# Where the first MoE 1 steps and the last weight conversions stand in chunk 1 of an attention and MoE kernel

## The chip, the cores and the metric

One core of a Trainium2 chip. The metric is the device time of one execution in microseconds, the median of several runs. Engines are named as the profile names them: PE (TensorE) with its weight loads PEld, DVE (VectorE), ACT (ScalarE), POOL (GpSimd), and SP, whose queue issues the DMAs. Each engine, and each DMA queue, takes its instructions in the order in which the program wrote them.

## The reference

Three stages run one after the other, all in float32 (the weights of the two MoE stages come as 8-byte values):

```python
for t in range(768):                       # 4 batches x 8 heads, state 40 x 40
    y[:, :, t] = einsum('bhd,bhde->bhe', rt, state)
    Sa = einsum('bhde,bhe->bhd', state, at)
    state = state * wt - outer(Sa, bt) + outer(vt, kt)
x = y as [3072, 320]
h = x @ w_in                               # MoE 1: 320 -> 2048 -> 320
x = (h * clip(h + 3, 0, 6) / 6) @ w_out
out = ((x @ w_a) * (x @ w_b)) @ w_out2     # MoE 2: 320 -> 1536 -> 320
```

## The kernel before

**Attention.** The 768 steps are cut into 12 chunks of 64, and `window(j)` lists the steps of chunk j. A chunk's recurrence is turned into small matmuls and one triangular solve. `op_a(j + 1, 0)` and `op_a(j + 1, 1)` (L474) make the scores of the next chunk: 64 matmuls each on PE (L484), two copies of the diagonal blocks to AB on ACT (L487) and two masked copies on DVE (L491). `t_load(j + 1)` (L498) sends AB through memory into the layout of the solve (`scr`, then `TA`; L504, L507), and `t_start(j + 1)` runs the solve on POOL (L518, L521). One window later `t_store(j)` (L526) copies a part of the result on ACT (TA, L531), stores it (L534 to L536) and loads it back as NY and AB (L540 to L542); `merge_y(j)` (L544, matmuls L550) is the first step that needs it. After it come `merge_z`, `op_c`, `op_d`, `op_g`, `op_e`, `op_f` and `op_sd`, and with `op_b(j + 1)` (L576, matmuls L581, copies RH L582) the next window begins. POOL does nothing but solves from chunk 1 on.

**MoE 1.** Chunk j's output (256 tokens) goes through memory: `xt_move(j)` (L673) loads it back transposed, `prep(j)` (`moe1_x`, L286) splits it into xh (ACT, L290) and xl (DVE, L291), and then 8 `up` steps and 8 `down` steps follow. An `up(i)` is 16 matmuls (L311), then in turn ACT (g, L316), DVE (product, L317), ACT (gh, L132) and DVE (gl, L133). A `down(i)` is 12 matmuls (L331 to L333). They stand in one list `mq` in the order prep 0, up 0, up 1, down 0, up 2, down 1, ..., up 7, prep of the next chunk, down 6, down 7, up 0 of the next chunk, and so on. `MOE[j]` says ahead of which steps of window j the next entry of that list is issued; windows 2 to 9 have the same 16 places, two of them at 2 and 7. What is left after window 11 is issued in a loop of its own ahead of MoE 2 (L1045).

**Weights of MoE 1.** They are converted and split into two parts on the way. While `room["wide"]` holds, up to three or four pieces are in work at once; the first `xt_move` flushes them (L675) and from there on each `conv1.go()` is one narrow pass of up to 192 columns: load to `ws` (two buffers), ACT (L79), five DVE instructions (L80 to L88), ACT (L263), DVE (L265). Seven such passes are left when window 1 begins. `WEIGHTS[j]` says ahead of which steps they are issued; an entry that finds nothing to convert issues nothing.

**Order around the change.** Window 1 begins with `xt_move(0)`. Its steps 0 and 1 are `op_b(1, .)`, 2 and 3 the loads for chunk 3, 4 and 6 `op_a(2, .)`, 8 and 9 `t_load(2)` and `t_start(2)`, 11, 12, 14 and 15 `op_kbt(2, .)`, 17 `merge_y(1)`, 18 `merge_z(1)`, 22 and 23 `op_c`, 38 `op_f(1, 1)`, 41 and 42 `op_sd(2, .)`.

Of the kernel before, what the change touches and what calls it, by code (L numbers as in the profile page):

```python
# [29 lines left out]

MOE = {
    0: (),
    1: (13, 18, 18, 19, 21, 22, 26, 26, 34, 38, 39),
    **{j: (2, 7, 14, 14, 19, 20, 23, 25, 32, 34, 38, 39, 41, 45, 48, 49) for j in range(2, NCH - 2)},
    NCH - 2: (2, 5, 11, 11, 14, 15, 16, 17, 21, 23, 27, 28, 30, 34, 37, 38),
    NCH - 1: (3, 3, 3, 3, 3, 4, 6, 11, 11, 13, 13, 13, 19, 20, 23, 23, 23)}
WEIGHTS = {
    0: (0, 3, 6, 8, 10, 17, 18, 21, 22, 22, 26, 27),
    1: (1, 2, 4, 5, 10, 13, 16, 16, 33, 36)}
EARLY = NCH - 6  # L40
WCOLS = 256
STORE_1 = 25
RANGE = 7
INV_SCALE = 1.0e9

HALVES = ((0, 0), (1, 64))
# [50 lines left out]
def attention_and_moe(ctx, tc, t, flag):  # L97
# [283 lines left out]
    def setup_first():  # L381
        for q, eng in ((32, ve), (96, gp)):
            eng.memset(raw[q:q + 32], 1.0)
            eng.memset(raw[q:q + 32].rearrange("q (p t) -> q p t", p=NP)[:, :, 0:1], 0.0)
        load_kb(0)
        load_w(0)
        ve.memset(seg, 0.0)
        ve.memset(seg.rearrange("q (p t) -> q p t", p=4)[:, :, 0:1], 1.0)
        for q in (32, 96):
            gp.memset(LB[0][q:q + 32, q // 64], 0.0)  # L390
        load_a(0)
        for q in (32, 96):
            ve.memset(LB[1][q:q + 32, q // 64], 0.0)
        gp.memset(TN2, 0.0)
        make_identity(nc, ident)
        pad(KB)
        load_kb(1)
        pad(RV.rearrange("q a p c -> q (a p c)"))
        sp.dma_start(out=mask, in_=t["mask"])
        for z in n2:  # L400
            sp.dma_start(out=z.rearrange("a p s t -> (a p) s t")[:, :, 0:32], in_=TN2[0:32])
# [21 lines left out]
    def load_w(j):  # L423
        for ab, q in HALVES:
            sp.dma_start(out=raw[q:q + D], in_=t["we"][j, ab])

    def load_a(j):
        for ab, q in HALVES:
            sp.dma_start(out=LB[j % 2][q:q + D, ab], in_=t["ae"][j, ab])
# [9 lines left out]
    def load_vt(j):  # L439
        for ab, q in HALVES:  # L440
            sp.dma_start(out=VX[64 - q:128 - q, ab], in_=t["vte"][j, ab])
# [4 lines left out]
    def prep_w(j, k):  # L446
        rw = py["rw", k % 2] = a2.tile([128, 4, C], F32, tag="rw", name="rw")
        w = W[j % 3][:, 4 * k:4 * k + 4]
        ve.tensor_tensor_scan(out=w.rearrange("q p t -> q (p t)"), data0=raw[:, 260 * k:260 * k + 260], data1=seg,
                              initial=0.0, op0=ALU.mult, op1=ALU.add)  # L450
        ve.reciprocal(out=rw, in_=w[:, :, 1:65])  # L451

    def prep_a(j, eng=nc.vector, ps=slice(0, NP)):
        for ab in range(2):
            a_ = LB[j % 2][half(ab), ab, ps]
            eng.tensor_tensor(out=a_, in0=a_, in1=W[j % 3][half(ab), ps, 0:64], op=ALU.mult)
# [6 lines left out]
    def prep_kb(j, k, eng=nc.vector):  # L463
        kb = kb_of(j)[:, 4 * k:4 * k + 4].rearrange("q p (s c) -> q p s c", s=2)
        r1 = py["rw", k % 2]
        rw = r1.rearrange("q p (s c) -> q p s c", s=1)
        eng.tensor_tensor(out=kb, in0=kb, in1=rw.to_broadcast([128, 4, 2, C]), op=ALU.mult)

        square(r1, 1.0, stat[:, 8 * j + k:8 * j + k + 1])
# [4 lines left out]
    def op_a(j, hf, later=None):  # L474

        lb, AB, KB = LB[j % 2], ABs[j % 2], kb_of(j)
        p0 = 8 * hf
        pss = [bank().rearrange("q (p c) -> q p c", p=8) for _ in range(2)]
        for i in range(8):
            p = p0 + i  # L480
            for o in range(2):
                for ab in range(2):
                    c = o ^ ab
                    mm(pss[ab][half(c), i], KB[rows(ab), p, 64 * c:64 * c + 64], lb[rows(ab), ab, p],  # L484
                       start=True, stop=True)
        for ab in range(2):
            ac.copy(out=AB[half(ab), p0:p0 + 8], in_=pss[ab][half(ab)])  # L487

            def masked(ab=ab):
                o = half(1 - ab)  # L490
                ve.tensor_tensor(out=lb[o, ab, p0:p0 + 8], in0=pss[ab][o],  # L491
                                 in1=mask[o, None, :].to_broadcast([64, 8, 64]), op=ALU.mult)
            masked() if later is None else later.append(masked)
# [4 lines left out]
    def t_load(j, between=lambda: None):  # L498
        scr = dram.tile([2, 2, NP, 32, 32], F32, tag="scr", name="scr", bufs=2)
        AB = ABs[j % 2]  # L500
        for sub in range(2):
            for ab in range(2):
                r0 = 64 * ab + 32 * sub
                sp.dma_start(out=scr[sub, ab].rearrange("p s t -> s p t"),  # L504
                             in_=AB[r0:r0 + 32, :, 32 * sub:32 * sub + 32])
        between()
        sp.dma_start(out=TA2[t_half(j)], in_=scr.rearrange("u a p s t -> (u a p) s t"))  # L507
# [15 lines left out]
    def t_start(j):  # L523
        t_solve(t_half(j), gp)
# [434 lines left out]
    with tc.manual_schedule():  # L959
        gp.memset(stat, 0.0)  # L960
        setup_first()
        conv1.ahead()
        later = []
        for k in range(4):
            prep_w(0, k)
            prep_kb(0, k, gp)
            if k == 3:
                load_w(1)
                load_a(1)
            if k % 2:  # L970
                prep_a(0, ve, slice(4 * k - 4, 4 * k + 4))
                op_a(0, k // 2, later)
        t_load(0)
        setup_rest()
        load_vt(0)
        for k in range(4):
            prep_w(1, k)
            prep_kb(1, k, gp)
            later.pop(0)()
        prep_a(1)  # L980
        t_start(0)
        for hf in range(2):
            op_a(1, hf, later)
            for _ in range(2):
                conv1.go()
                later.pop(0)()

        def turn(j):
            for bk in range(4):
                op_kbt(j, bk)  # L990
                conv1.go()

        t_load(1, lambda: turn(0))
        t_start(1)
        load_w(2)
        load_kb(2)
        turn(1)
        load_rv(0)
        prep_sq(0)
        prep_sq(1)  # L1000
        conv1.go()
        t_store(0, conv1.go)

        streams = [moe1_stream(j) for j in range(NCH)]
        preps = [p for p, _, _ in streams]
        mq = [preps[0], streams[0][1][0]]
        for j, (_, ups, downs) in enumerate(streams):
            for i in range(1, 8):
                mq += [ups[i]] + (preps[j + 1:j + 2] if i == 7 else []) + [downs[i - 1]]
            mq += [downs[7]] + [u[0] for _, u, _ in streams[j + 1:j + 2]]  # L1010

        def moe_step():
            mq.pop(0)()
            while mq and mq[0] in preps:
                mq.pop(0)()

        first2, early = early2(), [0] * NCH
        for j in range(NCH):
            for f in window(j):
                if f == MOE_STEP:  # L1020
                    if j == 1 and mq[0] in preps:
                        mq.pop(0)()
                    else:
                        moe_step()
                elif f == WEIGHT and j >= EARLY:
                    early[j] += 1
                    if early[j] in (1, 4, 7):
                        next(first2, None)
                elif f == WEIGHT:
                    if conv1.todo or conv1.loaded or room["wide"]:  # L1030
                        conv1.go()
                else:
                    f[0](*f[1:])
        for _ in first2:
            pass
        at.close()
        c2 = ctx.enter_context(ExitStack())
        w2p = c2.enter_context(tc.tile_pool(name="w2", bufs=1, side="right", reuse_waits="tile"))
        xr = c2.enter_context(tc.tile_pool(name="x2", bufs=1, side="right", reuse_waits="tile"))
        left = []  # L1040
        w2 = Weights2(w2p, xr)
        load_x, trans, rest = moe2(w2, xr, lambda: left[0])
        decide = in_range()
        n = 0
        while len(mq) > 2:  # L1045
            moe_step()
            n += 1
            if n == RANGE:
                decide()
                load_x(0)  # L1050
            if n == RANGE + 5:
                trans(0)
                load_x(1)
        m1i.close()
        mq.pop(0)()
        trans(1)
        mq.pop(0)()
        m1w.close()
        left.append(c2.enter_context(tc.tile_pool(name="xl2", bufs=1, reuse_waits="tile")))
        rest()  # L1060
# [217 lines left out]
```

## Time and profile before

| | us |
|---|---|
| runs | 1282.98, 1289.79, 1292.96 |
| median | 1289.79 |
| the profiled execution | 1290.56 |
| its span, first to last instruction | 1288.7 |
| around the span | 1.9 |
| PE busy | 1099.9 (85%) |
| DVE busy | 827.2 (64%) |
| POOL busy | 470.6 (37%) |

A row of a timeline gives start and duration in microseconds, the engine, the line, the operation, what is written from what, shapes, count, and in brackets the idle time before it on its engine with what ended it.

### The profile page before, as it was taken

To read this page: it belongs to the slowest core of one execution; us is meant where nothing else is said; L and a number is where in the kernel's file an instruction comes from. 1 tells how busy PE (TensorE), PEld (TensorE's weight loads), DVE (VectorE), ACT (ScalarE), POOL (GpSimd) and SP (SyncE) were. 2 spreads that over 40 slices of the span, in tenths; PEclk is the share of its full clock that TensorE was granted. 3 is DMA by queue.
4 is the path that set the end of the run, shared out by engine and by line. 5 is a ranking of instruction groups with operands and counts; after the bars stand their busy time and mean duration, and the time that the engine had idled before them with its cause. 6 is when DMAs were issued, how large, how long until landed. Compare 5 with 4: busy or idle time off the path is not lost.

```text
span 1288.7 us, 34786 instructions
## 1 busy us (share of the span) xinstructions
PE 1099.9 (85%) x14826; PEld 1002.2 (78%) x14826; DVE 827.2 (64%) x1391; ACT 519.2 (40%) x1087; POOL 470.6 (37%) x797
## 2 busy tenths in 40 slices
PE   1213447988999998989999998999999999999997
PEld 1213336988998988979888998998888888888886
DVE  7899777565756566867777654345674775675332
ACT  1233344544554535455545554333443332332221
POOL 4789105556658484838465663000000000000000
PEclk9999857989999999999999999999999999999999
DMA  6254252333241505253433324132220110110111
GB/s 174 48 142 113 68 153 54 88 76 86 68 102 57 137 23 139 67 128 87 116 104 87 97 61 106 48 107 89 78 71 20 41 41 22 43 41 6 41 42 43
DMA packets 133858, 100.33 MB, mean 78 GB/s; under 512 B 87520, under 2 KB 121440, under 8 KB 131680
## 3 DMA queue, kind: packets, MB, share of 16 engines
q1 hardware_dynamic: 133696, 98.04, 28.0%
q8 instruction: 118, 1.93, 0.6%
q14 instruction: 44, 0.36, 0.1%
HBM read 75.13 MB, written 22.87 MB: 76 GB/s over the span
## 4 chain that ended last, share of the span: by engine, by line
PE 42%; DVE 16%; POOL 14%; DMA 11%; ACT 7%; issue 6%; SPq 3%; DVEq 0%; ACTq 0%; POOLq 0%
PE att L891 21%; POOL TN L521 7%; POOL TT L518 7%; PE up L311 4%; PE ac L915 3%; PE ac L914 3%; PE ac L913 3%; DMA KB<-in_kbe_dram 2%; DVE rw L451 2%; DMA scr<-AB 2%; DMA n<-TA 2%; PE dn L333 1%; DMA st<-in_w1o_dram 1%; PE dn L331 1%; DMA TA<-scr 1%
## 5 line engine op out<-in xcount | busy, mean ns | idle before, releaser
L518 POOL TENSOR_TENSOR TT<-TA,TN 64x31 f32<-64x31 f32 (+15 forms) x372 | 214.5, 576 | 264.2 <-DMA TA<-scr 235.8
L891 PE MATMUL att<-x2h,up 128*128 128x512 f32 x720 | 237.2, 394 | 0.0
L521 POOL TENSOR_TENSOR TN<-TN,TT 64x31 f32<-64x31 f32 (+15 forms) x372 | 224.2, 603 | 29.2
L891 PE MATMUL att<-x2l,up 128*128 128x512 f32 x432 | 170.4, 395 | 2.0 <-DVE x2l L876 2.0
L891 PEld LDWEIGHTS att<-x2h,up 128*128 128x128 f32 x720 | 135.0, 188 | 28.9
L331 PE MATMUL dn<-wo_h,gh 128*128 128x320 f32 x384 | 130.7, 340 | 13.3 <-ACT gh L132 13.3
L333 PE MATMUL dn<-wo_h,gl 128*128 128x320 f32 x384 | 124.6, 324 | 1.5 <-DVE gl L133 1.5
L332 PE MATMUL dn<-wo_l,gh 128*128 128x320 f32 x384 | 123.1, 321 | 0.0
L317 DVE SCALAR_TENSOR_TENSOR up<-g,up 128x512 f32<-128x512 f32 x96 | 66.3, 690 | 82.1 <-ACT g L316 81.9
L896 DVE TENSOR_TENSOR att<-att,asb 128x512 f32<-128x512 f32 x72 | 50.4, 700 | 97.5 <-PE att L891 80.5
L316 ACT ACTIVATE g<-up,bias 128x512 f32<-128x512 f32 x96 | 66.0, 688 | 114.0 <-PE up L311 111.5
L311 PE MATMUL up<-xh,wi_h 128*128 128x256 f32 x384 | 107.4, 301 | 3.1 <-ACT xh L290 3.1
L132 ACT CAST gh<-up 128x512 fp32r<-128x512 f32 x96 | 56.2, 586 | 129.4 <-DVE up L317 126.1
L133 DVE TENSOR_TENSOR gl<-up,gh 128x512 fp32r<-128x512 f32 x96 | 66.4, 691 | 65.1 <-ACT gh L132 65.1
L311 PE MATMUL up<-xh,wi_l 128*128 128x256 f32 x384 | 101.8, 286 | 0.0
L891 PEld LDWEIGHTS att<-x2l,up 128*128 128x128 f32 x432 | 81.1, 188 | 19.4 <-DVE x2l L876 3.5
L331 PEld LDWEIGHTS dn<-wo_h,gh 128*128 128x128 f32 x384 | 75.7, 197 | 18.1 <-ACT gh L132 14.6
L913 PE MATMUL ac<-dn,g2h 128*128 128x320 f32 x288 | 89.5, 311 | 0.0
L915 PE MATMUL ac<-dn,g2l 128*128 128x320 f32 x288 | 88.6, 308 | 0.1
L914 PE MATMUL ac<-dn,g2h 128*128 128x320 f32 x288 | 88.7, 308 | 0.0
L451 DVE RECIPROCAL rw<-W 128x256 f32<-128x256 f32 x48 | 84.2, 1753 | 3.2 <-ACT sq L461 0.2
L132 ACT CAST g2h<-att 128x512 fp32r<-128x512 f32 x72 | 42.2, 587 | 103.7 <-DVE att L896 101.7
(149 smaller groups left out, 2476.8 us busy)
## 6 DMA issues: line engine op xcount, KB each, us to landing
RV<-in_rve_dram SPq DMA_DIRECT2D x24, 320.0 KB
KB<-in_kbe_dram SPq DMA_DIRECT2D x22, 320.0 KB
st<-in_w1i_dram SPq DMA_DIRECT2D x13, 384.0 KB
raw<-in_we_dram SPq DMA_DIRECT2D x24, 162.5 KB
LB<-in_ae_dram SPq DMA_DIRECT2D x24, 160.0 KB
VX<-in_vte_dram SPq DMA_DIRECT2D x24, 160.0 KB
yt<-Y SPq DMA_DIRECT2D x48, 80.0 KB
x2d<-x SPq DMA_DIRECT2D x24, 160.0 KB
```

Of the source, the lines that this page charges most:

```text
L132: ac.copy(out=hi, in_=src)
L311: mm(u[:, e], a_, b_, start=(n == 0), stop=(n == len(seq) - 1))
L331: mm(acc, gh[:, e, c0:c0 + 128], wo_h[:, m], start=(m == 0), stop=False)
L332: mm(acc, gh[:, e, c0:c0 + 128], wo_l[:, m], start=False, stop=False)
L333: mm(acc, gl[:, e, c0:c0 + 128], wo_h[:, m], start=False, stop=(m == 15))
L451: ve.reciprocal(out=rw, in_=w[:, :, 1:65])
L518: eng.tensor_tensor(out=tv, in0=TA[:, 0:u, u:u + 1].to_broadcast([nr, u, n]), in1=TN[:, u:u + 1, u:32].to_broadcast([nr, u, n]), op=ALU.mult)
L521: eng.tensor_tensor(out=TN[:, 0:u, u:32], in0=TN[:, 0:u, u:32], in1=tv, op=ALU.subtract)
L891: mm(u, a_, b_, start=(n == 0), stop=(n == len(seq) - 1))
L913: mm(acc, gh[:, sl], w[:, 0], start=(i == 0), stop=False)
L914: mm(acc, gh[:, sl], w[:, 1], start=False, stop=False)
L915: mm(acc, gl[:, sl], w[:, 0], start=False, stop=(i == BLOCK - 1))
```

## The change

Three tables and one number of the code change. Chunk 1 gets 14 MoE 1 entries in place of 11, from step 5 on in place of step 13; its conversions stand at steps 0 to 13; the fallback decision and the first transposes for MoE 2 follow the shift in the last loop.

```diff
-    1: (13, 18, 18, 19, 21, 22, 26, 26, 34, 38, 39),
+    1: (5, 6, 8, 10, 13, 16, 18, 19, 21, 22, 26, 26, 34, 38),
...
-    1: (1, 2, 4, 5, 10, 13, 16, 16, 33, 36)}
+    1: (0, 0, 1, 2, 3, 5, 6, 8, 10, 13)}
...
-RANGE = 7
+RANGE = 5
...
-            if n == RANGE + 5:
+            if n == RANGE + 4:
                 trans(0)
```

Written out with the code's own lists, the head of window 1 is (pass = one narrow conversion):

```
before: xt_move 0 | op_b 0 | pass 1 | op_b 1 | pass 2 | loads | pass 3 | op_a 0 | pass 4 | op_a 1 |
        t_load, t_start | pass 5 | kbt 0, 1 | pass 6, prep | kbt 2, 3 | pass 7 | merge_y | up 0, up 1 |
        merge_z | down 0 | up 2 | down 1 | op_c 0, 1 | up 3, down 2 | ... | up 4 | ... | down 3 | op_f 1 | up 5
after:  xt_move 0 | passes 1, 2 | op_b 0 | pass 3 | op_b 1 | pass 4 | load | pass 5 | load | op_a 0 |
        pass 6, prep | pass 7, up 0 | op_a 1 | up 1 | t_load, t_start | down 0 | kbt 0, 1 | up 2 | kbt 2, 3 |
        down 1 | merge_y | up 3 | merge_z | down 2 | up 4 | down 3 | op_c 0, 1 | up 5, down 4 | ... | up 6 | ... |
        down 5 | op_f 1
```

All later windows take the list three entries further on at unchanged places. In windows 2 to 9, and at the like places of window 10, that puts at place 2 (behind `op_b`, ahead of `t_store`) `up 7` and the next chunk's prep where `down 4` stood, at place 7 (between the two `op_a`) `down 6` where `up 6` stood, and at place 32 (ahead of `op_g`) `up 3` where `down 0` stood. The last loop has three entries fewer (`up 6`, `down 5` and `up 7` of chunk 10 are done).

## Rows read from the trace of the kernel before

**Rows 1.** Stretch: us; busy (count) of PE, PEld, DVE, ACT, POOL; PEclk, DMA share, GB/s
```profile
183.00:204.00 21.00, 7.70 (x144) 6.39 (x144) 15.72 (x43) 8.27 (x24) 0.23 (x1) 0.50 0.46 121
```

**Rows 2.** Timeline of ACT in the head of window 1
```profile
184.39 0.37 ACT L79 ACTIVATE cv<-ws 128x192 f32<-128x192 f32 x1 [0.55 <-DMA ws<-in_w1o_dram]
191.05 0.30 ACT L263 CAST wi_h<-cv 128x128 fp32r<-128x128 f32 x1 [1.54 <-DVE cv L88]
195.00 1.18 ACT L487 COPY AB<-att 64x512 f32<-64x512 f32 x2
203.46 0.83 ACT L290 CAST xh<-xt 128x768 fp32r<-128x768 f32 x1
```

**Rows 3.** Timeline of PE there: op_a(2, 1), first matmuls of up 0 and up 1
```profile
187.30 1.98 PE L484 MATMUL att<-LB,KB 40*64 40x64 f32 x62 [2.93 <-ACT RH L582]
204.34 0.58 PE L311 MATMUL up<-xh,wi_h 128*128 128x256 f32 x1 [3.12 <-ACT xh L290]
207.92 0.41 PE L311 MATMUL up<-xh,wi_h 128*128 128x256 f32 x1
```

**Rows 4.** Timeline of POOL: first and last instruction of chunk 2's solve
```profile
203.77 0.28 POOL L518 TENSOR_TENSOR TT<-TA,TN 64x31 f32<-64x31 f32 x1 [68.53 <-DMA TA<-scr]
243.75 0.24 POOL L521 TENSOR_TENSOR TN<-TN,TT 64x31 f32<-64x31 f32 x1
```

**Rows 5.** Chain that ended last, in window 1: start, us, what (op_c; up 5)
```profile
221.56 1.99 PE att L590 x64
241.96 2.11 PE up L311 x16
```

**Rows 6.** Timeline of PE and ACT where window 2 begins
```profile
245.33 2.06 PE L581 MATMUL att<-VX,LB 128*64 128x40 f32 x64
245.60 0.58 ACT L132 CAST gh<-up 128x512 fp32r<-128x512 f32 x1 [0.76 <-DVE up L317]
249.65 2.03 ACT L531 COPY TA<-TN 32x1024 f32<-32x1024 f32 x1
```

**Rows 7.** Timelines of PE, ACT and SP where windows 3, 5 and 10 begin
```profile
306.07 2.06 PE L581 MATMUL att<-VX,LB 128*64 128x40 f32 x64
311.68 2.05 ACT L531 COPY TA<-TN 32x1024 f32<-32x1024 f32 x1 [1.19 <-POOL TN L521]
321.27 0.48 SPq L540 DMA_DIRECT2D NY<-n  x1
326.56 1.20 PE L550 MATMUL att<-NY,AB 32*32 32x32 f32 x64
...
438.11 0.48 SPq L540 DMA_DIRECT2D NY<-n  x1
440.36 1.19 PE L550 MATMUL att<-NY,AB 32*32 32x32 f32 x62 [0.79 <-DMA NY<-n]
...
726.77 2.06 PE L581 MATMUL att<-VX,LB 128*64 128x40 f32 x64
731.45 2.04 ACT L531 COPY TA<-TN 32x1024 f32<-32x1024 f32 x1
```

**Rows 8.** Waits of PE from 250 to 790 us: total us, times, longest
```profile
PE dn L331 <- ACT gh L132: 11.8, 6, 3.1
PE att L550 <- DMA NY<-n: 8.4, 6, 2.0
```

**Rows 9.** Timeline of DVE in window 4
```profile
392.82 0.70 DVE L467 TENSOR_TENSOR KB<-KB,rw 128x512 f32<-128x512 f32 x1 [5.39 <-DMA KB<-in_kbe_dram]
```

**Rows 10.** Chain that ended last, in the last loop: two up steps in succession
```profile
859.55 1.92 PE up L311 x16
863.23 1.92 PE up L311 x16
```

**Rows 11.** Stretches of window 2 and of window 7, columns as in rows 1
```profile
264.00:268.00 4.00, 4.00 (x51) 3.94 (x47) 0.76 (x1) 1.15 (x2) 0.00 (x0) 0.50 0.38 52
547.00:608.00 61.00, 54.82 (x1073) 51.18 (x1073) 45.36 (x67) 32.07 (x67) 35.42 (x60) 1.00 0.39 104
```

## The prediction

> **What bounds the kernel now.** I read the head of window 1 first, since only its order is rewritten by hand, and then the beginning of each later window, where the shift of three entries lands. In the busy times of the stretch from 183 to 204 us PE works 7.7 of 21 us, at a granted clock of 0.50, the 1.2 GHz level [rows 1]: this is the hole into which the change puts work. The timeline of POOL shows what the hole costs besides: chunk 2's solve begins at 203.77, after 68.53 us without work, and lasts until 243.99 [rows 4]. What it waits for is the second pair of AB copies, which ends on ACT at 196.18 [rows 2]; the 7.6 us from there to 203.77 are t_load's way through memory.
>
> From window 2 on two loops run side by side. One is the solve with its transfers. In the other PE waits for NY, merges, works through the window up to the next op_b, and ACT makes the TA copy, from whose result the next NY comes. The first row of such a pair: op_b ends at 308.13 and TA follows at 311.68, 1.19 us of that spent on the solve; eight windows on, op_b ends at 728.83 and TA follows at 731.45 [rows 7]. Over the eight windows 3 to 10 that way takes 2.6 to 4.0 us, 25.6 together. PE in its turn waits for NY in several windows, 8.4 us in all [rows 8]. Both loops are thus within a microsecond or two of being the slower one, so work added to either of them is not free. From window 11 on PE alone sets the end.
>
> **The change part by part. The tail.** Three entries leave the last loop: two ups and one down. There a pair of up and down takes 3.68 us (863.23 less 859.55), the up 1.92 of it [rows 10], so the three are worth 1.92 + 1.76 + 1.92 = 5.6 us of PE. Window 11 holds as many entries as before. Gain: 5.6.
>
> **The head of window 1.** On ACT the two AB pairs get more in front of them. Three passes, with the RH copies between, now take from 184.39 to 191.35, 2.3 us each [rows 2]. In the new order five passes precede the first AB pair: 184.4 + 5 x 2.3 = 196.0. That pair costs 1.2, the sixth pass 2.3 and, on DVE, the masked copies of the first pair about 1; with xh (0.83, [rows 2]) up 0 can begin at about 201.4. At 1.2 GHz its 16 matmuls took 3.58 us (204.34 to 207.92, [rows 3]); the long idle time before them leaves no reason for another clock, so it ends at 205.0. The seventh pass hides under it. Then op_a(2, 1) takes 1.98 [rows 3] and ends at 207.0, while g, product and gh of up 0 hold ACT until 207.1: up 5 began at 241.96 and its gh ended at 246.18 [rows 5, 6], 4.2 us of which 2.1 lie behind the matmuls. The second AB pair ends at 207.1 + 1.2 = 208.3, against 196.18: 12.1 us later. The solve moves by as much, to 243.99 + 12.1 = 256.1. Its result is fetched by the TA copy, which came 5.7 us after the solve's end, at 249.65 [rows 6], so only 256.3 - 249.65 = 6.7 us come through.
>
> PE must not be later than that. From 207.0 up to the end of op_b(2, .) it has 6 ups at 2.11, 6 downs at 1.76, the attention work of the stretch 221.56 to 247.39 [rows 5, 6] without its five MoE steps (25.8 - 3 x 2.11 - 2 x 1.76 = 16.0) and ahead of it the two merges at 1.2 [rows 7] and four transposes (an estimate by their size: 1.9 in all): 43.5 us, up to 250.5. PE is done before the solve; with the 5.1 us from the next step it reaches TA at 255.6. So the solve sets it, and the loss at the TA copy of window 2 is 6.7; its bounds are 3.1 (PE's own shift, if the solve catches up) and 10 (if each of the passes, up 0 and the clock cost a little more).
>
> The load of chunk 3's decays and of its `ae` stands behind more `ws` loads on SP, and its kb load moves with the transposes; what uses them stands behind op_a and behind merge_z on DVE, so I charge nothing, and their cover is the later solve itself.
>
> A sentence on the skill: Perfetto Trace Analysis, "Optimization Strategies", asks to keep the matmul engine at as high a utilization as possible, which by itself would count the three steps as 5.6 us gained and give 1285. The same section goes on to the engines that block the critical path, and the trace bears out that half: POOL's 68.53 us are blocked by ACT's order, and the change lengthens that.
>
> **Windows 2 to 10.** At place 2 stands up 7 with the next prep, ahead of t_store. ACT then has g, gh and xh in front of the TA copy. From op_b's end: 4.2 (up 5's way from its first matmul to the end of gh, [rows 5, 6]) + 0.83 (xh, [rows 2]) = 5.1 us, in place of 25.6 / 8 = 3.2. For the eight windows 3 to 10 this is 8 x 1.9 = 15.2 us, if PE waits for NY each time. Behind the TA copy on ACT stand the AB copies, so PE's banks and t_load wait as well. The xt that prep needs was loaded since the window before, and down 6 at place 7 takes g and gh of up 6 away from between the AB pairs; neither sets anything by the rows, since t_load is held by NY's and AB's loads on SP.
>
> Against it stands, first, window 3, where PE reaches merge_y at 326.56 without a wait: its last NY load was issued by 321.75, and such a load lands 1.8 us after its issue (438.59 to 440.36, [rows 7]), at 323.5, so 3.0 us are slack. Second, PE's waits for gh ahead of a down, 11.8 us in six windows [rows 8]: this is down 0 at place 32, whose up 0 has its product on DVE behind the wait for KB, 5.39 us in window 4 [rows 9]. At that place now stands an up, which needs no gh. What follows it, op_g, needs ACT's VX copies, which still stand behind a gh that waits for the same KB; so the gain lies between nothing and 11.8. I take half, 5.9, since an up of 2.1 us now fills a part of each such wait, and the next step inherits the rest. Sum of these windows: 15.2 - 3.0 - 5.9 = 6.3, with bounds of 0.4 (all of the 11.8) and 15.2 (no slack and no gain).
>
> **The end.** prep 11 stands three steps behind op_f(11, 1) where it stood seven; down 6 and down 7 (3.5 us) are between it and the first matmul that needs it, and I charge nothing. The fallback decision, one entry later, is a single matmul and three small DVE instructions.
>
> **Sum.** 6.7 + 6.3 - 5.6 = 7.4 us later than the profiled execution's 1290.56, which lies 0.8 above the median of the runs: 1298.
>
> **The rivals.** *Slower: TA is late in each window.* The place is ACT between RH and TA, the price 1.9 us in each of eight windows, with nothing given back: op_g inherits the whole wait for KB and NY is always last. Then 6.7 + 15.2 - 5.6 = 16.3, 1307. It decides, in the sense of over 1%, once less than about 4 of the 14.8 us that stand against it are got back. For it: PE's NY waits (8.4 us) are there now, so a later NY is felt. Against: the KB wait no longer has a down right behind it.
>
> *Hidden: PE's order is all that counts.* The later solve is caught up (3.1 at window 2) and the waits for gh go entirely (0.4): 3.1 + 0.4 - 5.6 = -2.1, 1288; with half of the NY waits gone besides, 1284. For it: the stretch with the idle PE is real. Against: the solve's 40 us cannot shrink and its start hangs on ACT's order alone.
>
> *Slower: the clock.* Behind the idle time of PE around merge_y in window 2 the granted clock was 0.50 from 264 to 268, the 1.2 GHz level, while window 7 stayed at 1.00 [rows 11]. If the longer wait for NY in windows 4 to 10 lets the clock fall each time, 4 us at half speed cost 2 us, 14 in seven windows: 1298 + 14 = 1312. The Trainium skill, TensorE: Matmul & The Clock Gate, "HAM oscillation", describes just such a loop, in which a transfer's wait returns PE to the lower clock in each pass; by that rule, this rival. The trace shows the fall in window 2 and none in window 7.
>
> **How the numbers follow.** The likeliest is the partial loss, 0.53, at 1298 with a range of its own from 1288 to 1305. TA late in each window has 0.22, the hidden case 0.18, the clock 0.07. The range 1284 to 1308 takes in the hidden case and the slower one up to its sum and leaves the clock out. About 1% (13 us, 1277 and 1303) is what a measurement of this kernel can tell from no change. Slower by over 1%: 0.19 from the first rival, the clock's 0.07 and 0.05 of the likeliest case, 0.31. Faster by over 1% needs all of the moved work's 5.6 us and most of the waits: 0.09, nearly all of it from the hidden case. Within 1%: 0.60.
>
> **What would show it.** Chunk 2's solve should begin near 216, with a POOL wait of about 80 us in front; the first MoE matmul near 201.4 at half clock; TA of window 2 near 256; the way from op_b's end to TA near 5 us in windows 3 to 10; the waits of dn for gh mostly gone, and longer waits for NY in their place. MoE 2 should begin some 7 us later than now. If the solve begins before 208, the head of the sum is wrong, and if TA to TA stays under 59 us on the mean, the windows are.

## The result, and the profile after

The changed kernel takes 1294.95 us in the median, the kernel before on the same chip 1287.70: the ratio is 1.0058, 95% interval [1.0042, 1.0073], 7.3 us slower. Forecast were 7.4 us and 1298 (counted from a single run of 1290.56), in the range 1284 to 1308, and "within 1%" as the likeliest class. The profiled execution has a span of 1293.2 us against 1288.7. That the forecast fits is in part luck: its head came out, its middle did not, as the part on the prediction shows.

The head of window 1 in the changed kernel, from the timelines of PE, ACT and POOL (start, duration, instruction, idle time before it):

```profile
201.08 0.58 PE L311 MATMUL up<-xh,wi_h 128*128 128x256 f32 x1 [22.20 <-ACT xh L290]
204.67 1.16 PE L484 MATMUL att<-LB,KB 40*64 40x64 f32 x64
206.71 1.19 ACT L487 COPY AB<-att 64x512 f32<-64x512 f32 x2
215.15 0.24 POOL L518 TENSOR_TENSOR TT<-TA,TN 64x31 f32<-64x31 f32 x1 [78.85 <-DMA TA<-scr]
257.15 1.93 ACT L531 COPY TA<-TN 32x1024 f32<-32x1024 f32 x1 [2.23 <-POOL TN L521]
```

These answer to [rows 2 to 4] and [rows 6]. Up 0 starts at 201.08, the second AB pair ends at 207.90 in place of 196.18, the solve starts at 215.15 in place of 203.77, and TA of window 2 comes at 257.15 in place of 249.65, held by the solve.

Where the 4.5 us between the two profiled executions arise is read off the TA copies, one in each window, and the first matmul of MoE 2 (all starts from the timelines; the differences are worked out). The last row has the same differences for a second profiled execution of the changed kernel:

| | TA w2 | w3 | w4 | w5 | w6 | w7 | w8 | w9 | w10 | w11 | MoE 2 |
|---|---|---|---|---|---|---|---|---|---|---|---|
| before | 249.65 | 311.68 | 371.60 | 429.95 | 488.85 | 548.85 | 609.93 | 670.84 | 731.45 | 787.73 | 877.00 |
| after | 257.15 | 315.06 | 373.00 | 430.75 | 487.14 | 550.50 | 614.30 | 679.30 | 739.37 | 796.96 | 882.31 |
| later by | 7.5 | 3.4 | 1.4 | 0.8 | -1.7 | 1.7 | 4.4 | 8.5 | 7.9 | 9.2 | 5.3 |
| second execution, later by | 7.2 | 3.4 | 3.7 | 2.8 | 1.5 | 5.1 | 7.8 | 10.4 | 10.9 | 10.0 | 8.6 |

In the first execution the 7.5 us of the head are given back by window 6, and more; then windows 6 to 8 lose 10.2; window 11 and the last loop give back 3.9. In the second these three are 5.6, 8.9 and 1.4 us: the signs are the same, and a size read off a single profile holds to some 4 us. What PE waits for shows the exchange. The changed kernel's waits of PE from 250 to 790 us (total us, times, longest):

```profile
PE att L571 <- DVE LB L491: 20.8, 9, 5.5
PE att L639 <- DVE GH L618: 11.4, 10, 3.2
PE att L655 <- ACT VX L592: 5.4, 6, 1.9
PE att L590 <- ACT AB L564: 5.3, 7, 1.5
```

The two waits of [rows 8], for gh ahead of a down and for NY, are gone. In their place stand a wait of the transposes (L571) for the masked copies of the scores, which come behind the later TA copy, and a longer wait of op_f (L639) for GH's mask: 11.4 us in place of 2.8. Three waits of 3.2, 2.7 and 3.2 us, one in each of the windows 6 to 8, make up most of it. The one in window 7 of the changed kernel, on DVE and PE:

```profile
595.50 0.37 DVE L133 TENSOR_TENSOR ws<-cv,ws 128x160 fp32r<-128x160 f32 x1 [0.39 <-ACT ws L132]
595.79 0.68 DVE L640 TENSOR_TENSOR Y<-att,W 104x512 f32<-104x512 f32 x1
596.39 0.68 DVE L317 SCALAR_TENSOR_TENSOR up<-g,up 128x512 f32<-128x512 f32 x1
597.72 0.69 DVE L133 TENSOR_TENSOR gl<-up,gh 128x512 fp32r<-128x512 f32 x1 [0.65 <-ACT gh L132]
598.33 1.28 DVE L618 TENSOR_TENSOR GH<-att,mask 128x512 f32<-128x512 f32 x2
599.06 0.33 PE L639 MATMUL att<-GH,KBT 128*64 128x64 f32 x2 [2.74 <-DVE GH L618]
```

On DVE the end of a conversion of MoE 2's weights, a Y, the product and gl of up 5, and only then the mask. Before, a down stood at that place (41), and PE waited for GH not over 0.7 us at a time.

PE's clock moved with the waits. Busy times from 250 to 490 and from 490 to 790 us (columns as in [rows 1], the clock is the third figure from the right), the kernel before first, then the change:

```profile
250.00:490.00 240.00, 227.46 (x4340) 214.17 (x4330) 145.63 (x188) 119.06 (x241) 149.96 (x256) 0.96 0.33 84
490.00:790.00 300.00, 280.45 (x5315) 262.65 (x5315) 209.87 (x305) 155.29 (x320) 181.25 (x319) 0.98 0.37 98
```

```profile
250.00:490.00 240.00, 223.16 (x4434) 209.41 (x4433) 151.52 (x192) 123.88 (x246) 156.65 (x273) 0.99 0.35 91
490.00:790.00 300.00, 271.52 (x5055) 253.98 (x5055) 202.98 (x295) 145.97 (x304) 178.62 (x312) 0.95 0.35 90
```

An estimate from these rows: what the lower clock takes from PE is 4% of 240 us before and 1% in the change, 9.6 against 2.4 us, and then 2% of 300 us before and 5% in the change, 6 against 15 us. So much of what windows 2 to 5 gain and of what the later windows lose goes with the clock. It fell behind each of the three long waits for GH (PE's rows of windows 6 and 8; the granted clock is 0.79 from 532 to 540, from 596 to 604 and from 664 to 672):

```profile
535.19 0.33 PE L639 MATMUL att<-GH,KBT 128*64 128x64 f32 x2 [3.21 <-DVE GH L618]
663.94 0.33 PE L639 MATMUL att<-GH,KBT 128*64 128x64 f32 x2 [3.21 <-DVE GH L618]
```

By estimate each such fall takes 0.21 of 8 us, 1.7 us, on top of the wait. In the second execution the clock was 0.96 from 250 to 490 and 0.95 from 490 to 790, and its windows 2 to 5 give back less.

### The profile page after: what moved, and what is told of

It reads as the page before. It is cut to its first block, busy times and chain, and to the rows that moved or that the text cites. A ratio compares the mean times of both kernels' runs of the same rounds, so it can differ in the third digit from the quotient of the medians.

```text
span 1293.2 us, 34833 instructions
## 1 busy us (share of the span) xinstructions
PE 1089.2 (84%) x14826; PEld 992.3 (77%) x14826; DVE 829.1 (64%) x1391; ACT 520.0 (40%) x1087; POOL 471.5 (36%) x797
## 4 chain that ended last, share of the span: by engine, by line
PE 55%; DVE 18%; DMA 8%; ACT 8%; issue 5%; POOL 3%; SPq 2%; DVEq 0%; ACTq 0%; POOLq 0%
PE att L891 21%; PE up L311 9%; DMA KB<-in_kbe_dram 3%; PE ac L915 3%; PE ac L914 3%; PE ac L913 3%; PE dn L331 3%; PE dn L333 2%; PE dn L332 2%; DVE up L317 2%; ACT TA L531 2%; DVE rw L451 2%; POOL TN L521 1%; POOL TT L518 1%; DVE W L449 1%
## 5 line engine op out<-in xcount | busy, mean ns | idle before, releaser
L311 PE MATMUL up<-xh,wi_h 128*128 128x256 f32 x384 | 110.7, 309 | 22.2 <-ACT xh L290 22.2
L331 PE MATMUL dn<-wo_h,gh 128*128 128x320 f32 x384 | 127.9, 333 | 1.5 <-ACT gh L132 1.5
L333 PE MATMUL dn<-wo_h,gl 128*128 128x320 f32 x384 | 121.9, 317 | 0.7 <-DVE gl L133 0.7
L311 PEld LDWEIGHTS up<-xh,wi_h 128*128 128x128 f32 x384 | 75.0, 195 | 26.9 <-ACT xh L290 22.4
```

Source lines behind the costliest of these rows:

```text
L311: mm(u[:, e], a_, b_, start=(n == 0), stop=(n == len(seq) - 1))
L331: mm(acc, gh[:, e, c0:c0 + 128], wo_h[:, m], start=(m == 0), stop=False)
L333: mm(acc, gl[:, e, c0:c0 + 128], wo_h[:, m], start=False, stop=(m == 15))
```

## The experiments

All ratios are to the kernel before, run beside each kernel on the same chip, with the 95% interval. The medians come from several chips, on which the kernel before took 1287.26 to 1293.06, so the ratios are what can be compared. TA and other times come from one profiled execution of each kernel.

| kernel | median us | ratio to before |
|---|---|---|
| the change | 1294.95 | 1.0058 [1.0042, 1.0073] |
| the change, again | 1297.40 | 1.0077 [1.0051, 1.0102] |
| shift only (old head) | 1298.30 | 1.0039 [1.0010, 1.0069] |
| head only (old order later) | 1292.83 | 1.0015 [0.9988, 1.0043] |
| TA copy first | 1299.29 | 1.0061 [1.0037, 1.0084] |
| mask first | 1284.84 | 0.9961 [0.9930, 0.9991] |
| mask first, again | 1286.96 | 1.0001 [0.9981, 1.0020] |
| mask first, old head | 1287.92 | 1.0004 [0.9983, 1.0025] |
| conversion earlier | 1299.76 | 1.0061 [1.0033, 1.0088] |
| mask first, conversion earlier | 1297.75 | 1.0060 [1.0026, 1.0093] |
| mask first, passes late | 1306.24 | 1.0122 [1.0077, 1.0168] |
| all three | 1316.82 | 1.0213 [1.0161, 1.0265] |
| before, ae load later | 1295.59 | 1.0064 [1.0039, 1.0089] |

**Shift only.** Against the changed kernel, the old head, with 14 entries:

```diff
-    1: (5, 6, 8, 10, 13, 16, 18, 19, 21, 22, 26, 26, 34, 38),
+    1: (13, 18, 18, 19, 21, 22, 24, 26, 26, 28, 30, 34, 38, 39),
-    1: (0, 0, 1, 2, 3, 5, 6, 8, 10, 13)}
+    1: (1, 2, 4, 5, 10, 13, 16, 16, 33, 36)}
```

> The changed kernel with chunk 1's old head: conversions where they were, no MoE 1 entry before step 13, but still 14 entries in the window, so all later windows are shifted by three entries as in the change. Theory (the later solve of chunk 2 and the PE order meet within a microsecond or two at window 2): chunk 2's solve begins at 204 again, but PE has 3 more steps in a stretch that is full, so op_b of chunk 2 ends some 5 us later than before (about 252) and the TA copy of window 2, behind up 7 and the prep, comes at about 257; from there all is as in the changed kernel, 7 us slower than before, within 2 us of the change. Rival (the head alone costs the time): TA of window 2 near 250 and the time within 2 us of before.

From its timelines:

```profile
203.81 0.24 POOL L518 TENSOR_TENSOR TT<-TA,TN 64x31 f32<-64x31 f32 x1 [66.94 <-DMA TA<-scr]
243.61 0.24 POOL L521 TENSOR_TENSOR TN<-TN,TT 64x31 f32<-64x31 f32 x1
249.21 2.06 PE L581 MATMUL att<-VX,LB 128*64 128x40 f32 x64
256.14 2.01 ACT L531 COPY TA<-TN 32x1024 f32<-32x1024 f32 x1
```

The solve is back at its old time, and its result lies ready for 12.3 us, because op_b ends at 251.27 and TA stands behind up 7 and the prep. TA comes as late as in the change. So the late solve and the extra steps are not two prices that add up: window 2 is 6.5 us late with the extra steps alone, 6.7 with the late solve alone (next experiment) and 7.5 with both. The kernel is slower than before by 0.4%, and the rival (the head alone) falls.

**Head only.** The changed head, but 11 entries and the old order of all later windows:

```diff
-    1: (5, 6, 8, 10, 13, 16, 18, 19, 21, 22, 26, 26, 34, 38),
+    1: (5, 6, 8, 10, 21, 22, 26, 26, 34, 38, 39),
-RANGE = 5
+RANGE = 7
-            if n == RANGE + 4:
+            if n == RANGE + 5:
```

> The changed head of chunk 1 (conversions at steps 0 to 13, prep and up 0 ahead of the second scores), but 11 entries in the window as before, the last seven at their old places, so later windows have their old order. Theory: chunk 2's solve begins at about 216 and TA of window 2 comes at 257, some 7 us late, with nothing taken off the last loop; of these up to 4 us come back in windows 2 and 3, since the loads that run beside the stores of the solve are over by then: 3 to 7 us slower than before. Rival (the hole is filled, so PE work is saved): within 1 us of before or faster by up to 5.

The solve starts at 214.87 and TA of window 2 comes at 256.30, 6.7 late as the head's sum had it. But from there to the next TA it is 57.1 us in place of 62.0 before, and the last TA, at 788.60, is 0.9 behind that of before. The measured loss, 0.15%, can't be told from none; it lies just under the 3 us expected at least. A late solve of 6.7 us in window 2 is thus mostly given back a window later. The rival, that a filled hole saves PE work, is not refuted by the time alone: 0.15% lies between the two expectations.

**TA copy first.** The changed kernel with the order of PE untouched, ACT's altered:

```diff
-    **{j: (2, 7, 14, ...
+    **{j: (5, 7, 14, ...
-    NCH - 2: (2, 5, 11, ...
+    NCH - 2: (3, 5, 11, ...
```

> The changed kernel with one thing altered: in windows 2 to 10 up 7 and the prep are issued behind t_store, so that ACT makes the TA copy ahead of g, gh and xh; the order of PE is the same. Theory A (the way from op_b's end to TA costs 1.9 us a window): it falls from 5.0 to about 3, and the kernel is 5 to 12 us faster than the change. Theory B (the later TA copy costs nothing, because its store then runs when the loads of the window are over): the way falls, but TA to the first NY load grows from 4.0 to 4.9 us back to 5.4 to 8, and the time stays within 2 us of the change.

Window 3 in the changed kernel, then in this one (ACT's TA copy, SP's issue of its store and of the first NY load):

```profile
315.06 1.98 ACT L531 COPY TA<-TN 32x1024 f32<-32x1024 f32 x1
317.07 0.31 SPq L536 DMA_DIRECT2D n<-TA  x1
319.44 0.32 SPq L540 DMA_DIRECT2D NY<-n  x1
```

```profile
313.78 2.05 ACT L531 COPY TA<-TN 32x1024 f32<-32x1024 f32 x1 [1.88 <-POOL TN L521]
315.86 0.31 SPq L536 DMA_DIRECT2D n<-TA  x1
320.74 0.32 SPq L540 DMA_DIRECT2D NY<-n  x1
```

The store that took 2.4 us from its issue to the issue of the load behind it takes 4.9. Over windows 3 to 10 the way from op_b's end to TA falls from 4.9 to 1.0 to 3.8 us, and TA to the first NY load grows from 4.0 to 5.0 to between 5.4 and 8.6. The time does not move: theory B. Measured from op_b's end to the first NY load the mean of windows 3 to 10 is 9.8 us in the kernel before, 9.2 in the change and 8.9 here, whatever stands between. One thing else moved: PE's wait for LB rose from 20.8 to 25.7 us, so a small gain of the earlier TA copy may be hidden behind it.

**Before, ae load later.** To see whether that store is slow because of the loads beside it, the kernel before with the loads of 320 KB moved from ahead of t_store to behind the solve's start:

```diff
-            + ... + on(nx2, (load_a, j + 2)) + on(j > 1, (t_store, j))
+            + ... + on(nx2, (idle,) if j else (load_a, j + 2)) + on(j > 1, (t_store, j))
-   ... (t_load, j + 1), (t_start, j + 1)) + pw(0)
+   ... (t_load, j + 1), (start_and_load, j + 1)) + pw(0)
```

> The kernel before with one thing altered: the two loads of the `ae` part (320 KB a window) are issued behind the solve's start in place of ahead of t_store; MoE 1 and the conversions as before. Theory (a store of the solve takes longer when the loads of the window run beside it; a later TA copy therefore costs nothing): TA to the first NY load falls from 5.4 to 9.3 to about 4 to 6, TA to merge_y by one to two, and the kernel is up to 8 us faster than before. Rival (what matters is where TA stands, not the loads): TA to NY stays above 5.4 in most windows and the time within 2 us.

TA to the first NY load stayed at 4.7 to 7.7 us in windows 2 to 10, so the cause is not shown. Its mean over windows 3 to 10 fell from 6.6 to 6.1 us, and op_b's end to that load from 9.8 to 8.7, which is in the direction of the theory and small. The load now stood right ahead of the KB load on SP, and the price is seen in the waits of DVE (first) and of PE:

```profile
DVE KB L467 <- DMA KB<-in_kbe_dram: 47.2, 8, 7.2
```

```profile
PE dn L331 <- ACT gh L132: 25.3, 7, 4.8
```

KB's wait was 32.1 us before and the downs' wait 11.8 [rows 8]: the kernel is 0.6% slower.

**Mask first.** The changed kernel with one entry of each window moved behind op_e(j, 1):

```diff
-    **{j: (2, 7, 14, 14, 19, 20, 23, 25, 32, 34, 38, 39, 41, 45, 48, 49) ...
+    **{j: (2, 7, 14, 14, 19, 20, 23, 25, 32, 34, 38, 39, 43, 45, 48, 49) ...
-    NCH - 2: (2, 5, 11, 11, 14, 15, 16, 17, 21, 23, 27, 28, 30, 34, 37, 38),
+    NCH - 2: (2, 5, 11, 11, 14, 15, 16, 17, 21, 23, 27, 28, 32, 34, 37, 38),
```

> The changed kernel with one entry of windows 2 to 10 moved from ahead of op_e(j, 1) to behind it, so that DVE makes GH's second mask ahead of that up's product and gl. Theory (windows 6 to 8 lost 10 us against before because GH's mask stood behind a conversion, a Y, an up's product and gl): PE's waits for GH, 11.4 us in all, fall under 3, windows 6 to 8 take 60 to 62 us each in place of 63 to 65, and the kernel is 5 to 9 us faster than the change. Rival (these windows are bound by DVE and the waits only move): within 2 us of the change, the waits turning up at op_g or op_c.

Its wait of PE for GH, and the same wait (as in [rows 8]) of the change in a second run:

```profile
PE att L639 <- DVE GH L618: 4.0, 6, 1.4
```

```profile
PE att L639 <- DVE GH L618: 7.9, 9, 3.2
```

Windows 6 to 8 take 61.0, 62.0 and 63.7 us in place of 63.4, 63.8 and 65.0; the kernel before takes 60.0, 61.1 and 60.9. So about half of these windows' loss comes back. The repetition beside the change on one chip:

> The kernel with the mask first once more, beside the change on the same chip: 0.993 to 0.999 of before, 8 to 13 us faster than the change.

> The change itself, beside the others on the same chip: 1.004 to 1.008 of before.

1286.96 against 1297.40 us, 10 us: this one entry's place is worth as much as the whole loss of the change on that chip, where the kernel before took 1287.26. The first ratio, 0.9961, was not found again (1.0001), so the mask-first kernel is level with before and no more is claimed for it. How the place makes 10 us is shown only in part. In the repetition windows 6 to 8 take 186.3 us in place of 190.9, and PE's wait for GH is 3.4 in place of 7.9, but its wait for VX is 7.4 in place of 3.2. The mean granted clock from 250 to 790 us is 0.97 in place of 0.96, an estimate of 5 us. The same move was not tried on the kernel before, where PE waits 2.8 us for GH in all.

**Mask first, old head.** The shift-only kernel with the same entry moved:

> The kernel with chunk 1's old head and 14 entries (shift only), with the mask first in windows 2 to 10. Theory (the two orders of chunk 1's head are worth the same, because PE is as late with the old one as the solve is with the new one): TA of window 2 near 256 as in the shift-only kernel, and the time within 3 us of the kernel with the new head and the mask first, 0.992 to 0.999 of before. Rival (filling the hole early is what pays): 4 to 8 us slower than that one.

1.0004 against 1.0001 on the same chip, TA of window 2 at 257.02: the new head and the old one are worth the same once the later windows are alike.

**Conversion earlier.** In windows 6 to 10 the second conversion step goes ahead of the fourth prep_kb (the change, then the mask-first kernel):

```diff
-                    if early[j] in (1, 4, 7):
+                    if early[j] in (1, 2, 7):
```

> The changed kernel with one conversion of MoE 2's weights per window (windows 6 to 10) moved from ahead of op_f(j, 0) to ahead of the fourth prep_kb, so that it no longer stands on DVE in front of the Y, the product and gl that precede GH's second mask; MoE 1 as in the change. Theory (the wait for GH in windows 6 to 8 comes from the conversion and the up together): the waits for GH, 11.4 us in the change, fall under 4, and the kernel is 4 to 10 us faster than the change. Rival (the up alone holds the mask): waits stay over 8 us and the time within 2 us.

> Mask first and the conversion moved as well. If both act on the same wait, this is within 2 us of the kernel with the mask first; if the conversion also lengthens windows 6 to 9 in other ways (they take 61 to 64 us there against 56 to 58 in windows 2 to 5), it is 3 to 8 us faster.

In the first of the two, the waits of PE:

```profile
PE dn L331 <- ACT gh L132: 11.5, 4, 3.9
PE att L655 <- ACT VX L592: 6.7, 5, 3.3
```

The wait for GH is down to 0.3 us, so the conversion did its part in it; but downs wait for gh again and op_g for VX, and the time stays that of the change. (This profile is of the slowest of 13 executions, 1310.74 us against a median of 1299.76.) With the mask first it is 0.6% slower than before, so moving the conversion undoes what the other move gains. Here the waits only moved, as the rival of the mask-first kernel had it.

**Passes late.** The mask-first kernel with the seven conversion passes behind t_load(2):

```diff
-    1: (0, 0, 1, 2, 3, 5, 6, 8, 10, 13)}
+    1: (10, 11, 13, 16, 19, 22, 24, 26, 28, 30)}
```

> The kernel with the mask first (one entry of windows 2 to 10 behind op_e(j, 1)), and the seven conversion passes moved from ahead of chunk 2's scores to behind t_load(2) and t_start(2); MoE 1 entries as in the change. Theory A (the head's delay is given back in window 2, as the head-only kernel suggests): chunk 2's solve begins near 203, 9 to 10 us earlier, TA of window 2 comes 3 to 7 us earlier, but the time changes by less than 3 us against the kernel with the mask first, since PE's own work then sets window 2. Theory B (the conversions in front cost what TA of window 2 loses): 5 to 9 us faster than the kernel with the mask first.

The solve starts at 199.42, 4 us ahead of the kernel before, and yet:

```profile
PE att L550 <- ACT KBT L574: 11.3, 1, 11.3
PE att L561 <- ACT NY L553: 8.9, 2, 8.6
PE att L616 <- ACT Pt L603: 6.0, 1, 6.0
```

These are the waits of PE from 204 to 270 us. ACT stands in the middle of a pass, up to 5.9 us for DVE's part of it, and its copies for PE stand behind it. DVE's part is longer here: other DVE work stands in it, and its instructions themselves take longer while POOL solves. The same instruction on the same shape, in the change with POOL idle, then here during the solve and after its end (the solve ends at 237.68):

```profile
202.19 0.29 DVE L82 SCALAR_TENSOR_TENSOR cv<-cv,ws 128x128 int32<-128x128 int32 x1
```

```profile
210.47 0.71 DVE L82 SCALAR_TENSOR_TENSOR cv<-cv,ws 128x128 int32<-128x128 int32 x1
242.98 0.29 DVE L82 SCALAR_TENSOR_TENSOR cv<-cv,ws 128x128 int32<-128x128 int32 x1
```

Busy times from 204 to 256 us (us; PE, PEld, DVE, ACT, POOL; PEclk, DMA share, GB/s), this kernel first, then the change:

```profile
204.00:256.00 52.00, 31.53 (x490) 29.39 (x492) 37.46 (x61) 17.43 (x48) 30.71 (x55) 0.70 0.11 32
```

```profile
204.00:256.00 52.00, 50.83 (x1113) 48.30 (x1111) 34.79 (x44) 26.39 (x57) 36.31 (x59) 1.00 0.22 58
```

TA of window 2 comes at 272.68, 15.5 later than in the change. Neither theory held: the passes cost less in front of the scores, where only the solve waits for them and POOL is idle, than among the steps that feed PE during the solve. Which of the two, the copies queued behind the passes or the slower DVE, costs more is not separated. All three moves together cost 2.1%, which is not the sum of the single effects that was expected:

> Mask first, the conversion moved and the seven passes behind t_load(2). The sum of the single effects: the better of the mask-first kernels, and up to 3 us less if the head's delay is given back, 5 to 9 less if it is not.

## Why the prediction came out, point by point

**The head was right.** Up 0 at 201.08 (201.4 expected), the AB pair at 207.90 (208.3), the solve at 215.15 (near 216), op_b's end at 248.59 (250.5), TA 7.5 us late (6.7), set by the solve. One step in it failed: up 0 at half clock was right, 3.6 us from its first matmul to op_a's, but op_a itself ran in 1.16 and not in 1.98, as the clock had risen by then (granted 0.50 from 200 to 204 us, 1.00 from 204.6).

**Its consequence was wrong.** The 6.7 us were entered in the sum as a loss that lasts. Head only shows that they are given back, 4.9 us of them in window 2: 0.15% at the end. The mask-first kernels with the old and the new head fit this, with window 2 as late (7.4 and 8.5 us) and the time level with before, though they have the shorter tail as well.

**Windows 2 to 10: the mechanism was there, its price was not.** The way from op_b's end to TA is 4.86 to 5.00 us in windows 3 to 10, 5.1 expected. But the term of 15.2 us charged 1.9 us a window for it on the premise that PE waits for NY each time, and longer waits for NY were named as a sign. They did not come: the 8.4 us of before went to none. TA copy first shows no gain in time from taking the way back (1.0061 against 1.0058): the store behind a later TA is quicker by nearly as much. The trace of before hinted at it: the first NY load follows TA by 5.4 us in one window and 9.3 in another, so TA alone did not set it. Why the store is slow there stays open; the ae loads alone are not the cause, and the two stores of TN (128 KB each) that SP issues ahead of it were not moved.

**The waits for gh went entirely,** 11.8 us; half was counted. In their place PE waits 20.8 us for LB, which no term of the sum had; the text named it (AB copies behind TA, "so PE's banks and t_load wait as well") and charged nothing. In window 2 TA runs to 259.08, the AB copies and the masks behind it, and PE stands 5.5 us:

```profile
260.33 1.67 PE L571 MATMUL att<-ident,KB 104*128 104x104 f32 x8 [5.51 <-DVE LB L491]
```

**What was not seen:** at place 41 the shift put an up where a down had stood, and GH's mask behind its product and gl on DVE, with a conversion in front in windows 6 to 8. These windows lost 10.2 us (8.9 in the second execution); moving the one entry gave 10 us of time back, of which 5.5 and 4.6 us are seen in these windows. The rest of their loss stays open. The prediction followed places 2, 7 and 32 and not this one.

**The tail** gave 3.9 us of 5.6 in the one execution and 1.4 in the other.

So the sum 6.7 + 6.3 - 5.6 and the measured 7.5 + 1.7 - 3.9 agree roughly in the first and last terms and in the total by two errors that cancel: the middle held a gain of 9.2 us in windows 2 to 5 that was not expected and a loss of 10.2 in windows 6 to 8 that was not expected either. The fit of the total, 7.4 forecast and 7.3 measured, is luck to that extent. The gain goes with the waits that left (NY, gh) and with the clock, 0.96 before and 0.99 in the change from 250 to 490 us; no experiment separates the two.

**The rivals.** TA late in each window: its way was there in each window, its price in none. Hidden: the head's delay was caught up and the waits for gh went, as it says, but the delay only behind window 2, and the end was wrong. The clock: it fell in window 2, to 0.50 from 260 to 264 us behind the wait of 5.5 us for LB, in none of the windows 3 to 5, and at least once in each of the windows 6 to 10, behind waits for LB, GH and AB and not for NY. A wait of 1.89 us for LB at 490.40 was followed by a fall and one of the same length at 376.27 was not. The kernel before has such falls too, so that from 250 to 790 us the mean is 0.97 in both: the rival's mechanism was there, its 14 us were not, and by the estimate above it moved time from windows 2 to 5 to the later ones. The Trainium skill, TensorE: Matmul & The Clock Gate, "HAM oscillation", describes a loop in which the fall comes back in each pass; the trace agrees for windows 6 to 10 and not for 3 to 5. The busy PE that the Trainium skill, Perfetto Trace Analysis, "Optimization Strategies", asks for was had in the hole, and passes late shows how little a busy hole says by itself: there PE was busy 13.88 of the 21 us from 183 to 204 but only 31.53 of the 52 behind it, and the kernel was slower by 1.2%.

## What to carry to other kernels

When a list of steps is shifted against fixed places, go through every place and ask, engine by engine, what now stands ahead of the copy that PE waits for next; the one place not looked at cost as much here as the whole change. A copy that is made later is a loss only if what follows it was ready to take it: look whether the time behind it varies from pass to pass, and if it does, something else sets the end. Work that ties two engines together in short turns, as a conversion does, belongs where the copies of a busy PE don't queue behind it. And look at the granted clock of each stretch before a gain or a loss is put down to a wait alone: a wait of 3 us cost by estimate 1.7 us more through it here.

## What the runs showed of the hardware

The store of 128 KB behind the TA copy took 2.4 us from its issue to the load that waits for it in one kernel and 4.9 in another in the same window, with the same bytes; there it was the slower one that was issued sooner, and taking 320 KB of loads from ahead of it shortened op_b's end to that load by 1.1 us only, on the mean of eight windows. PE's clock was back at the upper level, 2.4 GHz, by the end of the first MoE step in the changed kernel: up 0's matmuls began 0.21 us apart, up 1's 0.12 us, and op_a's 64 between them took 1.16 us. One DVE instruction of a conversion pass took two to two and a half times as long while POOL's solve ran: L82 on 128x128 values took 0.29 us with POOL idle, 0.57 to 0.75 during the solve in passes late (0.59 in the kernel before), and 0.29 again after it.
